# One ScalarE instruction for both PSUM banks of a pair, the first modulation by blocks, a warm-up from a cleared tile, and new instruction orders

## The chip, the core and the metric

The kernel runs on one core of a Trainium2 chip. The metric is device time in microseconds (us) of one execution. A core has five engines that run side by side and meet at semaphores: TensorE (PE, matmuls), VectorE (DVE), ScalarE (ACT), GpSimd (POOL) and SyncE (SP, which issues most DMAs). Matmul results land in PSUM, which has 8 banks of 512 float32 columns for each of 128 partitions.

## The reference

One transformer block on 2048 tokens of width 512, modulated by a condition `c`: Infini-attention (32 heads of 16, four segments of 512 tokens, causal softmax inside a segment plus a linear memory of the earlier ones), and a squared-ReLU feed-forward part of width 1792.

```python
mod = silu(c) @ w_mod                       # sa, ca, ga, sb, cb, gb
h = layernorm(x) * (1 + ca) + sa
q, k, v = heads(h @ wq), heads(h @ wk), heads(h @ wv)
for s in range(4):                          # segments of 512 tokens
    p = softmax(q_s @ k_s.T * 0.25 + causal)
    a_mem = phi(q_s) @ M / (phi(q_s) @ z + 1e-6)
    o_s = g * a_mem + (1 - g) * (p @ v_s)
    M, z = M + phi(k_s).T @ v_s, z + sum(phi(k_s))
x = x + ga * (o @ wo)
h = layernorm(x) * (1 + cb) + sb
x = x + gb * (relu(h @ w1 + b1) ** 2 @ w2 + b2)
```

## The kernel before

The work is cut into 16 units: segment `s` and a quarter `cc` of the heads (8 heads, 128 columns of q and k), `u = 4 s + cc`. For each unit there are q and k (`qk`), for each segment v (`vproj`), then for each of two quads of four heads the row maxima (`a_quad`), the scores, their exponentials and the product with v (`b_quad`), and the memory (`mem`). The output projection (`wo_tile`) and the feed-forward part (`ffn1`, `ffn2`) follow. Operands are split into a high and a low part, and three matmuls stand for one.

Every piece of work is a node of a class `Plan`: an engine, a duration that the author guessed, the nodes it waits for, and the buffers that it takes (`get`) and gives back (`put`). `Plan.run` walks through the nodes in virtual time and so fixes which buffer a key has (`slot`) and at which virtual time a node starts; where a table `ORDER` names the nodes of an engine in sequence, that sequence is kept. The program is then written in the order of the virtual start times. What really waits for what is decided later, from the tiles that the instructions read and write: a semaphore wait is set wherever an instruction and an earlier one of another engine touch the same place. PSUM is handed out by `slot`, banks 0 to 7; the bank of a key is a tile of its own:

```python
def bank(key):
    if key not in TL:
        TL[key] = ps.tile([P, 512], F32, name=f"b{key[0]}", tag=f"bank{PL.slot[key]}")
    return TL[key]
```

TensorE works on half of its rows at a time in `qk`, `vproj`, `a_quad` and the scores: two matmuls of 64 rows run beside each other and write to two banks, a pair. ScalarE reads the two banks of a pair with two instructions: the exponentials (L1081), the copy of the first maxima (L942), the negated maxima (L976), the memory's reads (L1001, L1014) and v (L863, by 128 columns). VectorE takes the maxima in PSUM, in place (L909).

At the start TensorE multiplies a tile `msk` with itself (46 warm-up matmuls, `bwarm`, L562). The modulation's first two rows come by `mod_cols(1, ...)` (L584, L604, L606) and `mod_first(0, ...)` (L619, L625); the first layer norm (`ln1`) applies its statistics (L645), turns the tiles (L654), scales them by the modulation (L666, L668) and splits them into `HT`, from which the first `qk` reads (L782).

Of the kernel before, what the change touches and what calls it, by code (L numbers as in the profile page):

```python
# [8 lines left out]
F32 = mybir.dt.float32  # L9
# [9 lines left out]
P = 128  # L19
# [53 lines left out]
1107 1375 1229 1376 1121 1116 1045-1047 1399 1140 1400 1143 1401-1402 1134 1147 1404 1155 1242 1405 1126 1406 1150
1237 1407 1248 1137 1159 1234 1163 1160-1161 1253 1166 1539 1170 1540 1178 1271 1541-1542 1239 1471 1173 1544-1546
1244 1258 1547 1433 1446 1182-1184 1274 1277 1261 1284 1961-1962 1973-1974 1292 1416-1417 1256 1418-1419 1287 1280
1421 1263 1422 1452 1441 1423 1438 1424 1608 1460 1296-1298 1457 1300 1676 1307 1677 1303 1443 1678-1679 1310 1465
1315 1681-1682 1448 1683 1462 1475 1684 1570 1319 1478 1320-1321 1481 1578 1813 1488 1814 1491 1815 1467 1816 1589
1583 1484 1818-1819 1602 1496 1745 1820 1575 1612 1821 1580 1500 1615 1599 1504 1501-1502 1511 1597 1514 1585 1507
1519 1882 1707 1594 1523 1618 1717 1621 1524-1525 1625 1604 1720 1628 1712 1749 1633 1715 1726 1637-1639 1739 1641
1983 1648 1984 1656 1985 1722 1986 1651 1644 1734 1988-1989 1844 1990 1857 1991 1849 1752 1660-1662 2011 1852 2012  # L80
1755 2013-2014 1762 1765 1854 2016-2017 1770 1731 2018 1859 2019 1736 1863 2145-2146 1873 2083 2147-2148 1758 1876
1868 2150-2151 1741 2152-2153 2045 1871 1774-1776 1778 2028 1781 2029 1785 1788 2030-2031 1793 1878 2033 2064 2058
1797-1799 2034 1892 1899 2050 2035-2036 2053 1907 2273-2275 2055 1902 2276 2211 1895 2077 2278-2280 2069 2060 2281
2074 2192 1911-1913 1915 1922 2072 1918 2205 1930 1925 2079 2197 1934 2200 2173 2087 1935-1936 2094 2097 2401 2178
2402-2404 2102 2183 2090 2406-2407 2186 2408-2409 2181 2339 2106 2188 2110 2113 1886 2107 2117 2202 2120 2108 1889
2301 2125 2309 2129 2215 2314 2218 2130-2131 2207 2311 2222 2225 2320 2230 2325 2234 2467 2235-2236 2306 2238 2241
2550-2552 2330 2245 2248 2553 2561-2564 2316 2253 2328 2429 2333 2257-2259 2439 2335 2343 2350 2346 2627-2630 2358
2434 2353 2362 2437 2448 2583-2586 2594-2595 2366 2442 2369 2363-2364 2373 2381 2444 2596-2597 2376 2456 2572-2573
2461 2453 2385-2387 2458 2471 2574-2575 2463 2474 2478 2481 2605-2606 2486 2490 2494 2497 2491-2492 2501 2504 2509
2607 2637-2638 2649-2650 2616 2608 2617 2513-2515 2618-2619 2863 2881 2803-2805 2865 2806 2867 2781 2868 2782-2783  # L90
2871 2784 2873-2874 2814-2815 2883 2816 2792 2817 2793 2885 2794-2795 2886 2990 2994 2989 2889 2891-2892 2899 2993
2992 2996 2991 2995 2901 2903 2845-2847 2855 2848 2856-2857 2904 2858 2907 2998-2999 2909-2910 3002 2825-2826 2917
2827-2828 3000 2919 2997 2921-2922 3001 2925 3004 2935 3003 3007 2927-2928 2937 2835-2838 3008 3005 2939 3006 3011
2940 2943 3012 3015 3066-3067 3009 2945-2946 2953 2955 3013 3016 3010 3080 2957 3020 2958 3081 3019 3017 2961
2963-2964 3014 2971 3021 3018 3022 3025 3024 2973 3023 3028 2975-2976 3106 3027 2979 3026 2981-2982 3029 3108 3030
3032 3110-3111 3042 3130 3033 3031 3039 3114 3036 3116-3117 3132 3134 3046-3047 3135 3048 3045 3049 3052 3055 3154
# [24 lines left out]
812-813 815 956 814 811 816 810 817 711 868 867 875 874 883 882 853-854 877 975 878 976 871 870 1207 1362 1209 1354
# [120 lines left out]
class Plan:  # L242
# [1386 lines left out]
```

## Time and profile before

| | |
|---|---|
| time, median of 3 runs | 771.0 us (767.26 to 775.83) |
| profiled execution | 772.31 us |
| its span, first to last instruction | 769.6 us |
| mean granted TensorE clock | 0.984 |
| busy: PE / DVE / ACT / POOL | 741.1 / 597.5 / 503.0 / 253.9 us |
| matmuls; ScalarE instructions | 6107; 977 |
| first `qk` matmul | 23.97 us |

The profile names instructions by line, engine, operation, and the tiles they write and read (`bpb<-ST`). Its first part gives the busy time of each engine, its chain the work that ended last, followed back from the end. A row of the groups has the count, busy time, mean nanoseconds of one, and the idle time ahead of it. Ends of matmuls are modelled, so that overlapping ones count once in a busy time and with their full length in a mean.

### The profile page before, as it was taken

The numbers are of one execution on the slowest core, as the hardware profiler recorded it, in microseconds if no ns is written. First come the engines' busy times: TensorE is split into PE (matmuls) and PEld (weight loads), VectorE is DVE, ScalarE is ACT, GpSimd is POOL, SyncE is SP. The second block draws the span as 40 slices with busy tenths as digits, with TensorE's granted clock in tenths as the row PEclk, the third lists the DMA queues.
The fourth block names the chain that finished last, engine by engine and source line by source line (L and its number), as shares of the span: only waits on it lengthen the run. The fifth ranks groups of instructions, "written<-read, shape, count | busy, mean of one in ns | idle before, by whom it ended". The sixth has DMA issues, their size and how long they took to land.

```text
span 769.6 us, 17112 instructions
## 1 busy us (share of the span) xinstructions
PE 741.1 (96%) x6107; PEld 579.8 (75%) x6107; DVE 597.5 (78%) x1459; ACT 503.0 (65%) x977; POOL 253.9 (33%) x351
## 2 busy tenths in 40 slices
PE   8999999999999999999999699999999999999998
PEld 4777657875777658765566478898999898899886
DVE  4585788978987878588778989999968776687542
ACT  1547778888887896788868445666657455645441
POOL 4445355457665674464667230100000000000000
PEclk9999899999999999999999799999999999999999
DMA  9664757446565766658887858655543243243401
GB/s 303 164 163 113 217 182 204 133 131 167 181 172 159 189 175 173 181 142 209 241 232 232 251 186 256 215 172 179 150 150 116 99 123 110 77 136 96 151 1 55
DMA packets 102141, 126.69 MB, mean 165 GB/s; under 512 B 18981, under 2 KB 54569, under 8 KB 102058
## 3 DMA queue, kind: packets, MB, share of 16 engines
q1 hardware_dynamic: 101906, 125.49, 55.9%
q8 instruction: 48, 0.79, 0.4%
q14 instruction: 35, 0.29, 0.1%
q10 hardware_dynamic: 152, 0.13, 0.1%
HBM read 70.59 MB, written 27.99 MB: 128 GB/s over the span
## 4 chain that ended last, share of the span: by engine, by line
PE 77%; DMA 6%; ACT 6%; SPq 4%; DVE 3%; issue 2%; POOL 1%; DVEq 0%; ACTq 0%; POOLq 0%
PE bqk L792 7%; PE bpf L1573 7%; PE bpf L1572 7%; PE bpf L1571 7%; PE bpv L1123 6%; PE bv L871 6%; PE ba L904 5%; PE bpb L1064 5%; PE bhy L1510 3%; PE bhy L1512 3%; PE bhy L1511 3%; ACT pt L1081 3%; SPq L846 3%; PE bhx L1510 2%; PE bhx L1512 2%; PE bhx L1511 2%
## 5 line engine op out<-in xcount | busy, mean ns | idle before, releaser
L909 DVE CUSTOM_DVE_ANT_0 ba<-ba,msk 128x384 f32<-128x384 f32 (+2 forms) x384 | 185.8, 542 | 48.1 <-PE ba L904 43.4
L1081 ACT ACTIVATE pt<-bpb 128x512 f32<-128x512 f32 x320 | 169.7, 610 | 20.3 <-PE bpb L1064 17.6
L792 PE MATMUL bqk<-HT,WQK 64*128 64x512 f32 x720 | 100.8, 396 | 0.6 <-POOL hinge_s L526 0.6
L1068 POOL TENSOR_SCALAR_AFFINE_SELECT pt<-pt 128x512 f32<-128x512 f32 x128 | 80.1, 649 | 49.2 <-ACT pt L1081 40.9
L1571 PE MATMUL bpf<-W,ST 128*128 128x512 f32 x224 | 89.1, 398 | 0.3 <-ACT ST L1555 0.3
L1573 PE MATMUL bpf<-W,ST 128*128 128x512 f32 x224 | 88.8, 396 | 0.5 <-DVE ST L1558 0.5
L1572 PE MATMUL bpf<-W,ST 128*128 128x512 f32 x224 | 88.7, 396 | 0.0
L1456 ACT CAST ST<-SG 128x768 fp32r<-128x768 f32 (+1 forms) x56 | 51.9, 940 | 54.5 <-PE bhy L1511 51.0
L1064 PE MATMUL bpb<-ST 64*128 64x256 f32 (+2 forms) x512 | 79.9, 353 | 5.7 <-ACT pt L1081 1.8
L904 PE MATMUL ba<-ST 63*128 63x256 f32 (+2 forms) x512 | 78.2, 355 | 3.9 <-DMA ST<-SG 1.3
L792 PEld LDWEIGHTS bqk<-HT,WQK 64*128 64x128 f32 x720 | 72.8, 185 | 10.2 <-POOL hinge_s L526 1.0
L1123 PE MATMUL bpv<-pt,VT 128*32 128x512 f32 (+3 forms) x1024 | 78.8, 437 | 0.7 <-POOL pt L1068 0.6
L1064 PEld LDWEIGHTS bpb<-ST 64*128 64x128 f32 x512 | 52.1, 188 | 26.3 <-ACT pt L1081 7.4
L904 PEld LDWEIGHTS ba<-ST 63*128 63x128 f32 x512 | 51.8, 188 | 25.8 <-ACT pt L1081 9.0
L1459 DVE TENSOR_TENSOR ST<-SG,ST 128x768 fp32r<-128x768 f32 (+1 forms) x56 | 61.2, 1098 | 7.1 <-ACT ST L1456 7.1
L1209 POOL TENSOR_TENSOR X1L<-X1L 128x512 f32<-128x512 f32 x40 | 52.8, 1323 | 27.6 <-DMA X1L<-o_gate 22.8
L1549 ACT ACTIVATE AC<-AC,b1c 128x512 f32<-128x512 f32 x56 | 38.1, 718 | 28.8 <-DVE AC L1531 28.6
L871 PE MATMUL bv<-WVO,HT 64*128 64x512 f32 x384 | 56.0, 399 | 0.6 <-DVE xt L668 0.4
L1123 PEld LDWEIGHTS bpv<-pt,VT 128*32 128x32 f32 x1024 | 27.8, 109 | 36.8 <-issue 25.6
L909 DVE DVE_READ_ACCUMULATOR2_ANT mx<- 128x1 f32 x384 | 53.6, 140 | 0.0
L1558 DVE TENSOR_TENSOR ST<-AC,ST 128x1024 fp32r<-128x1024 f32 x28 | 34.2, 1222 | 21.2 <-ACT ST L1555 21.1
L1573 PEld LDWEIGHTS bpf<-W,ST 128*128 128x128 f32 x224 | 42.1, 188 | 10.9 <-DVE ST L1558 1.0
(201 smaller groups left out, 1710.0 us busy)
## 6 DMA issues: line engine op xcount, KB each, us to landing
ST<-SG SPq DMA_DIRECT2D x192, 128.0 KB
SG<-s_dram SPq DMA_DIRECT2D x21, 512.0 KB
SG<-in_B_w SPq DMA_DIRECT2D x35, 256.0 KB
o_raw<-oraw SPq DMA_DIRECT2D x16, 512.0 KB
X1L<-o_raw SPq DMA_DIRECT2D x28, 256.0 KB
X1L<-o_gate SPq DMA_DIRECT2D x28, 256.0 KB
wm<-in_w_mod SPq DMA_DIRECT2D x20, 256.0 KB
xt<-in_A_x SPq DMA_DIRECT2D x16, 256.0 KB
```

The source lines that it names most:

```text
L792: m = nc.tensor.matmul(bank(("qk", u, w)), W3(w, k, x, cc * P, (cc + 1) * P)[z], HT[z, y, k], start=(ph == 0 and k == 0 and i == 0), stop= ...
L871: m = nc.tensor.matmul(bank(("v", s, t)), HT[z, x, k, t * P:(t + 1) * P], WVO[z, k, y], start=(ph == 0 and k == 0 and i == 0), stop=(ph == ...
L904: nc.tensor.matmul(dst[:, c0:c0 + n], ST[b:b + 63, 0, sl, qt * P:(qt + 1) * P], ST[b:b + 63, 1, sl, :n], start=True, stop=True)
L909: nc.vector.tensor_tensor_reduce(i, i, msk[:, 512 - n:], scale=1.0, scalar=-3e38, op0=ALU.add, op1=ALU.max, accum_out=o)
L1064: nc.tensor.matmul(dst, ST[b:b + 64, 1, sl, kb * P:(kb + 1) * P], ST[b:b + 64, 0, sl, q0:512], start=True, stop=True)
L1068: nc.gpsimd.affine_select(out=ap, in_=ap, pattern=[[0, ap.shape[1]], [1, P]], compare_op=ALU.is_ge, fill=0.0, base=0, channel_multiplier=-1)
L1081: ns = [act(512, lambda j=j: nc.scalar.activation(buf("PPP"[n], pt)[:, i + j], bank(keys[j]), AF.Exp, scale=0.25), pr[slot] + 0.01 + 0.001 ...
L1123: nc.tensor.matmul(bank(o)[32 * hq:32 * hq + 32, q0:q0 + src.shape[1]], v[:, a:a + 32], src, start=start, stop=stop, tile_position=(0, 32 ...
L1459: nc.vector.tensor_tensor(TL[kd][:, 1, o:o + b - a], raw(k)[:, a:b], TL[kd][:, 0, o:o + b - a].bitcast(F32), op=ALU.subtract)
L1571: nc.tensor.matmul(p, rh, FF["W2"][:, f, 0], start=(f == 0), stop=False)
L1572: nc.tensor.matmul(p, rh, FF["W2"][:, f, 1], start=False, stop=False)
L1573: nc.tensor.matmul(p, rl, FF["W2"][:, f, 0], start=False, stop=(f == NF - 1))
```

## The change

All of PSUM becomes one tile `PB` of 8 banks. `bank(key)` is a slice of it, and `banks(keys)` a view of two banks, a slice with the distance of the two as its step. The six reads of a pair by ScalarE become one instruction each. Where a node takes two banks, the lower one goes to the first key.

```diff
+    PB = ps.tile([P, 8, 512], F32, name="PB")
+
     def bank(key):
-        if key not in TL:
-            TL[key] = ps.tile([P, 512], F32, name=f"b{key[0]}", tag=f"bank{PL.slot[key]}")
-        return TL[key]
+        return PB[:, PL.slot[key]]
+
+    def banks(keys):
+        a, b = (PL.slot[k] for k in keys)
+        return PB[:, a:b + 1:b - a]
...
+        two = [key for pool, key in n.get if pool[0] == "#"]
+        if len(two) == 2 and self.slot[two[0]] > self.slot[two[1]]:
...
-            ns = [act(512, lambda j=j: nc.scalar.activation(buf("PPP"[n], pt)[:, i + j], bank(keys[j]), AF.Exp, scale=0.25),
-                      pr[slot] + 0.01 + 0.001 * j, after=[k], put=[keys[j]]) for j in (0, 1)]
+            ns = [act(1024, lambda: nc.scalar.activation(buf("PPP"[n], pt)[:, i:i + 2], banks(keys), AF.Exp, scale=0.25),
+                      pr[slot] + 0.01, after=[k], put=keys)]
...
-        cp = [act(512, lambda j=j: nc.scalar.copy(buf("ac", ac)[:, j], bank(keys[j])), pr[0] + 0.01 + 0.001 * j, after=[first],
-                  put=[keys[j]]) for j in (0, 1)]
+        cp = [act(1024, lambda: nc.scalar.copy(buf("ac", ac), banks(keys)), pr[0] + 0.01, after=[first], put=keys)]
...
-                nc.tensor.transpose(bank(b[r])[:16, z], TL[mx][z], ident[z, z])
+                nc.tensor.transpose(bank(b[r])[:16, 0:64], TL[mx][z], ident[z, z])
```

The same is done to the copies of v (256 columns of two banks), of the memory's reads (two lines) and of the negated maxima. The start and the planner's constants:

```diff
-    RARE, COLD, NEAR, LATE, RING = 2.3, 3.4, 0.12, 0.1, 8
+    RARE, COLD, NEAR, LATE, RING = 1.8, 3.4, 0.12, 0.1, 8
-    FREE = {"PE": 2.0, "ACT": 2.6, "DVE": 2.7, "POOL": 2.4, "SP": 0.8, "NIL": 0.0}
+    FREE = {"PE": 1.2, "ACT": 2.6, "DVE": 2.7, "POOL": 2.4, "SP": 0.8, "NIL": 0.0}
...
+    wz = const.tile([P, P], BF, name="wz")
+    nc.vector.memset(wz, 0.0)
...
-        pe("F", 0.22, lambda: nc.tensor.matmul(bank(wk_), msk[:, :P], msk, start=True, stop=True), 50.0,
+        pe("F", 0.22, lambda: nc.tensor.matmul(bank(wk_).rearrange("p (a n) -> p a n", a=4), wz, wz[:, None, :].to_broadcast([P, 4, P]), start=True, stop=True), 50.0,
...
-    n_ca = mod_cols(1, CA, 1.0, PR0 + 0.1, pool="P")
-    n_sa = mod_first(0, SA, 0.0, PR0 + 0.2)
-    MODC = {CA: [n_ca, n_sa]}
+    def mod_block(j):
+        c = slice(j * P, (j + 1) * P)
+        ld = [sp(lambda m=m: nc.sync.dma_start(buf("P", keys_m[m])[:, :, c],
+                                               wmod[:, m * D + j * P:m * D + (j + 1) * P].rearrange("(k p) n -> p k n", p=P)),
+                 PR0 + 0.1 + 0.01 * j + 0.001 * m, 200000, get=() if j else [("P", keys_m[m])]) for m in (0, 1)]
+        def mm():
+            for m in (0, 1):
+                for k in range(KD):
+                    nc.tensor.matmul(bank(b_m)[:, 2 * j + m:2 * j + m + 1], TL[keys_m[m]][:, k, c], cs[:, k:k + 1],
+                                     start=k == 0, stop=k == KD - 1)
...
+        return dve(2, lambda: nc.vector.tensor_tensor(modc[:, 0:2, j], bank(b_m)[:, 2 * j:2 * j + 2], one, op=ALU.add),
+                   PR0 + 0.13 + 0.01 * j, after=[n], put=[b_m])
+    MODC = {CA: [mod_block(j) for j in range(KD)]}
```

With this the scaling of columns block `k` waits for its own block of the modulation, and the first `qk` group for the first two parts of `HT`, its third step for the others. The tables of `ORDER` are all written anew; they begin

```diff
     "PE": """
-16 43 31 47 22 40 50 44 59 38 3 54 49 57 25 39 35 52 19-20 17 36 61 33 76 42 27 30 46 71 28 21 37 73 34 53 78 48 80 82
+16 29 18 20 45 28 52 39 21 44 59 3 35 55 22 25 61 50 37 36 23 58 49 56 48 32 26-27 38 40 54 51 69 43 46 73 90-91
```

The following rows are the built programs' instructions in sequence, with the semaphores each waits for in brackets (`Activation_49` counts ScalarE's instructions, `DVE_49` VectorE's, `PE_49` TensorE's, `Pool_49` GpSimd's). Before, on TensorE, in segment 0 where q and k of unit 1 (L792), v (L871) and the first maxima (L904) are interleaved:

```order
L871 MATMUL bv<-WVO,HT 128x512 x6
L792 MATMUL bqk<-HT,WQK 128x512 [waits Pool_49]
L792 MATMUL bqk<-HT,WQK 128x512 x5
L871 MATMUL bv<-WVO,HT 128x512 x6
L904 MATMUL ba_710<-ST 128x256 [waits DVE_49]
L904 MATMUL ba_711<-ST 128x256 [waits Activation_49]
```

The change, at the same work (q and k are L798 now, v L877, maxima L909):

```order
L877 MATMUL PB<-WVO,HT 128x512 x6
L909 MATMUL PB<-ST 128x512 [waits Activation_49]
L909 MATMUL PB<-ST 128x512
L798 MATMUL PB<-HT,WQK 128x512 [waits Pool_49]
L798 MATMUL PB<-HT,WQK 128x512 x5
L798 MATMUL PB<-HT,WQK 128x512 [waits Activation_49]
L798 MATMUL PB<-HT,WQK 128x512 x5
L798 MATMUL PB<-HT,WQK 128x512 [waits Activation_49]
L798 MATMUL PB<-HT,WQK 128x512 x5
```

The 48 matmuls of a unit's q and k add into the same two banks; two of its groups of six, in the midst of this sum, now begin with a wait for ScalarE.

On TensorE a little later, where the first scores (L1064, now L1066) come among q and k of the next unit, before:

```order
L904 MATMUL ba_934<-ST 128x512 [waits Activation_49]
L792 MATMUL bqk<-HT,WQK 128x512 [waits Pool_49]
L792 MATMUL bqk<-HT,WQK 128x512 x11
L1064 MATMUL bpb<-ST 128x256 [waits Activation_49] x2
L1064 MATMUL bpb<-ST 128x384 x2
L904 MATMUL ba_967<-ST 128x256 [waits DVE_49]
```

and with the change:

```order
L798 MATMUL PB<-HT,WQK 128x512 x6
L798 MATMUL PB<-HT,WQK 128x512 [waits Activation_49]
L798 MATMUL PB<-HT,WQK 128x512 x5
L909 MATMUL PB<-ST 128x256 x2
L909 MATMUL PB<-ST 128x384 x2
L1066 MATMUL PB<-ST 128x256 x2
```

Here, too, a group of the same sum has a wait for ScalarE that stood nowhere in it before.

On ScalarE, the exponentials of unit 0's first quad, before (L1081 for each bank, beside the copies of v, L863):

```order
L863 COPY VT_150<-bv 128x8x16
L1081 ACTIVATE pt<-bpb 128x512 [waits PE_49]
L1081 ACTIVATE pt<-bpb 128x512 [waits PE_49,Pool_49]
L1081 ACTIVATE pt<-bpb 128x512 [waits PE_49]
L1081 ACTIVATE pt<-bpb 128x512
L1081 ACTIVATE pt<-bpb 128x512 [waits PE_49] x2
```

and with the change (L1083 and L869):

```order
L869 COPY VT_152<-PB 128x16x16 [waits PE_49]
L1083 ACTIVATE pt<-PB 128x1024 [waits DVE_49]
L1083 ACTIVATE pt<-PB 128x1024 [waits DVE_49,PE_49]
L1083 ACTIVATE pt<-PB 128x1024 [waits PE_49]
L1083 ACTIVATE pt<-PB 128x1024 [waits DVE_49,PE_49]
```

Each row of 1024 columns stands for two of 512, and three of these four wait for VectorE besides, which none of the rows before does.

More of the change, by code (lines that the diff above doesn't have):

```diff
@@ L313, in run @@
             heapq.heappush(ev, (free[e], k, None, 0))
-        k, todo, idle, cold, rare = 0, len(self.nodes), free["PE"], 0.0, 0.0
+        k, todo, idle, cold, rare = 0, len(self.nodes), free["PE"], self.START, 0.0
         while todo:
@@ L607, in mod_cols @@
                    pr + 0.05, after=[n], put=[b])
-    def mod_first(m, slot, plus, pr):
-        key, b = ("wmod", m), ("modc", m)
-        n = None
-        for k in range(KD):
-            ld = sp(lambda k=k: nc.sync.dma_start(buf("P", key)[:, k], wmod[k * P:(k + 1) * P, m * D:(m + 1) * D]),
-                    pr + 0.001 * k, 175000, get=() if k else [("P", key)])
-            def mm(k):
-                for j in range(KD):
-                    nc.tensor.matmul(bank(b)[:, KD * j + k:KD * j + k + 1], TL[key][:, k, j * P:(j + 1) * P], cs[:, k:k + 1],
-                                     start=True, stop=True)
-            n = pe("F", 0.9, lambda k=k: mm(k), pr + 0.02 + 0.001 * k, after=[n_cs, ld, n], get=() if k else [("#D", b)],
-                   put=[key] if k == KD - 1 else (), act=0.05)
-        def out_():
-            nc.vector.tensor_reduce(modc[:, slot, :], bank(b)[:, :KD * KD].rearrange("p (j k) -> p j k", k=KD), axis=AX.X, op=ALU.add)
-            if plus:
-                nc.vector.tensor_scalar(modc[:, slot, :], modc[:, slot, :], plus, None, op0=ALU.add)
-        return op("DVE", 0.15 if plus else 0.08, out_, pr + 0.05, after=[n], put=[b])
     def ln_stats(xt, mv):
@@ L649, in ln_transposed, with need @@
         b = [("lnq", sc, s, i, j) for j in (0, 1)]
+        def need(k):
+            return MODC[sc][k:k + 1] if sc == CA else MODC[sc]
         def turn(h):
@@ L697, in block_kernel @@
     load_x(0, PR0)
-    n_ca = mod_cols(1, CA, 1.0, PR0 + 0.1, pool="P")
-    n_sa = mod_first(0, SA, 0.0, PR0 + 0.2)
-    MODC = {CA: [n_ca, n_sa]}
+    one = const.tile([P, 2], F32, name="one")
+    nc.vector.memset(one[:, 0:1], 0.0)
+    nc.vector.memset(one[:, 1:2], 1.0)
+    n_blk = []
+    keys_m, b_m = [("wm", 0, 0), ("wm", 1, 0)], ("modc", 0)
+    def mod_block(j):
[8 more added lines that the diff above has]
+                                     start=k == 0, stop=k == KD - 1)
+        n = pe("F", 0.9, mm, PR0 + 0.12 + 0.01 * j, after=[n_cs, *ld], get=() if j else [("#D", b_m)], put=keys_m, act=0.05)
+        if j == 0:
+            n_blk.append(n)
+        else:
+            n_blk[0].outs.append(n)
+            n.left += 1
+        return dve(2, lambda: nc.vector.tensor_tensor(modc[:, 0:2, j], bank(b_m)[:, 2 * j:2 * j + 2], one, op=ALU.add),
+                   PR0 + 0.13 + 0.01 * j, after=[n], put=[b_m])
+    MODC = {CA: [mod_block(j) for j in range(KD)]}
     HTN = {}
@@ L887, in vproj @@
             HUSE[s].append(n)
-            for t in (t0, t0 + 1):
-                for cc in range(4):
-                    u = 4 * s + cc
-                    VN[u].append(act(128, lambda t=t, cc=cc: cp(t, cc), pr[t] + 0.02 + 0.001 * cc,
-                                     after=[n, *VUSE[u - NV], *(VTN[u:u + 1])], put=[("v", s, t)]))
+            for cc in range(4):
+                u = 4 * s + cc
+                VN[u].append(act(256, lambda t0=t0, cc=cc: cp(t0, cc), pr[t0] + 0.02 + 0.001 * cc,
+                                 after=[n, *VUSE[u - NV], *(VTN[u:u + 1])], put=[("v", s, t0), ("v", s, t0 + 1)]))
     MXN = {}
@@ L973, in turn_m @@
                 z = slice(64 * r, 64 * r + 64)
-                nc.tensor.transpose(bank(b[r])[:16, z], TL[mx][z], ident[z, z])
+                nc.tensor.transpose(bank(b[r])[:16, 0:64], TL[mx][z], ident[z, z])
         n = pe("R", 0.06, turn_m, p_tail, after=reds, get=[("#D", k) for k in b], put=[mx])
-        n = [act(64, lambda r=r: nc.scalar.mul(buf("mt", mt, F32R)[:, 64 * r:64 * r + 64], bank(b[r])[:16, 64 * r:64 * r + 64], -1.0),
-                 p_tail, after=[n], get=() if r else [("mt", mt)], put=[b[r]]) for r in (0, 1)]
+        n = [act(128, lambda: nc.scalar.mul(buf("mt", mt, F32R).rearrange("p (r n) -> p r n", r=2), banks(b)[:16, :, 0:64], -1.0),
+                 p_tail, after=[n], get=[("mt", mt)], put=b)]
         sl = (4 * u + 2 * qd) % NSLOT
@@ L1000, in mem @@
             MRD[u] = [n]
-            n = [act(512, lambda r=r: nc.scalar.copy(buf("oraw", ar)[:4 * VP, r], bank(bs[r])[:4 * VP, :]), pr[0] + 0.01, after=[n], put=[bs[r]])
-                 for r in (0, 1)]
+            n = [act(1024, lambda: nc.scalar.copy(buf("oraw", ar)[:4 * VP], banks(bs)[:4 * VP]), pr[0] + 0.01, after=[n], put=bs)]
             AMN[u] = sp(lambda: nc.sync.dma_start(o_raw[u][2 * P:].rearrange("(r p) n -> p r n", r=2), TL[ar][:4 * VP]), pr[0] + 0.02, 290000, lat=1.35,
@@ L1013, in mem @@
             n = pe("R", 0.24, tr, pr[2], after=[PHN[u, 1], PKN.get(u - 1)], get=[("#D", k) for k in b] + [("pk", pk)], put=[f])
-            n = [act(256, lambda r=r: nc.scalar.copy(buf("pk", pk).rearrange("p (t n) -> p t n", t=4)[:, :, 64 * r:64 * r + 64],
-                                                     bank(b[r])[:, 0:256].rearrange("p (t n) -> p t n", t=4)), pr[2] + 0.01,
-                     after=[n], put=[b[r]]) for r in (0, 1)]
+            n = [act(512, lambda: nc.scalar.copy(buf("pk", pk).rearrange("p (t r n) -> p r t n", t=4, r=2),
+                                                 banks(b)[:, :, 0:256].rearrange("p r (t n) -> p r t n", t=4)), pr[2] + 0.01, after=[n], put=b)]
             def upd():
```

283 lines of the change are left out of this document (129 added, 154 removed), and 36 rows, old and new, of the table ORDER.

## The prediction

> **What bounds the kernel now.** I read the page's busy shares and its chain first, then busy time by stretches, then the chain inside one stretch.
>
> ```profile
> PE 741.1 (96%) x6107; PEld 579.8 (75%) x6107; DVE 597.5 (78%) x1459; ACT 503.0 (65%) x977; POOL 253.9 (33%) x351
> ...
> PE 77%; DMA 6%; ACT 6%; SPq 4%; DVE 3%; issue 2%; POOL 1%; DVEq 0%; ACTq 0%; POOLq 0%
> ```
>
> TensorE is busy for 96% of the span; the chain runs through it for 77%, through ScalarE for 6% (46 us), VectorE for 3% and GpSimd for 1%: 77 us in the three that wait for PSUM or feed TensorE.
>
> ```profile
> core 0: us, PE busy (x) PEld busy (x) DVE busy (x) ACT busy (x) POOL busy (x), PEclk, DMA share, GB/s
> 24.00:460.00 436.00, 414.95 (x4128) 296.31 (x4127) 351.62 (x1066) 325.49 (x733) 242.46 (x323) 0.98 0.66 183
> 460.00:740.00 280.00, 279.56 (x1746) 249.93 (x1745) 225.10 (x357) 164.77 (x226) 3.42 (x4) 1.00 0.45 142
> ```
>
> From 460 us on there is the feed-forward part: TensorE idles 0.4 us in 280. No instruction there reads two banks, so I take it as unchanged. What the change can move lies in the start (24 us) and the attention (24 to 460 us), where TensorE idles 21 us and ScalarE 110 us. In a middle stretch of the attention, 130 to 160 us, the chain is this:
>
> ```profile
> by line: PE bv L871 25.9%; PE bpv L1123 21.0%; PE bqk L792 18.8%; PE ba L904 12.5%; PE bpb L1064 10.1%; PE blnq L654 6.8%; PE bmr L997 2.6%; PE bmu L1022 1.0%; PE bpkt L1012 0.8%; PE bat L974 0.7%; issue 0.1%
> ...
> 141.55 1.38 PE bqk L792 x12
> ```
>
> It has nothing but TensorE in it. There a shorter ScalarE instruction gains nothing, and any time for which TensorE stands still is added to the end. Twelve half-row matmuls, six pairs, take 1.38 us: 0.23 us for a pair.
>
> **ScalarE's reads.** What they cost now, and the rows from which I take a read of 1024 columns:
>
> ```profile
> L1081 ACT ACTIVATE pt<-bpb 128x512 f32<-128x512 f32 x320 | 169.7, 610 | 20.3 <-PE bpb L1064 17.6 <-PE bat L974 0.6 <-PE ba L904 0.5
> ...
> L942 ACT COPY AC<-ba 128x512 f32<-128x512 f32 x64 | 36.9, 603 | 17.3 <-PE ba L904 17.1
> ...
> L1555 ACT CAST ST<-AC 128x1024 fp32r<-128x1024 f32 x28 | 29.5, 1052 | 3.9 <-PE bpf L1572 2.7 <-PE bwop L1265 0.5
> ...
> L1147 ACT COPY oraw<-bpv 128x512 f32<-128x512 f32 x32 | 19.1, 596 | 13.9 <-PE bpv L1123 9.9 <-ACT AC L942 2.0 <-issue 1.0
> ...
> L1001 ACT COPY ar<-bmr 80x512 f32<-80x512 f32 x24 | 13.7, 594 | 2.7 <-PE bmr L997 2.7
> L863 ACT COPY VT<-bv 128x128 f32<-128x128 f32 x64 | 13.5, 302 | 5.4 <-PE bv L871 2.8 <-PE ba L904 2.6
> L976 ACT ACTIVATE mt<-bat 16x64 fp32r<-16x64 f32 x64 | 10.3, 202 | 8.3 <-PE bat L974 7.7 <-ACT HT L674 0.4
> L1524 ACT COPY u<-bhx 128x256 f32<-128x256 f32 x28 | 10.2, 368 | 20.0 <-PE bhx L1512 15.4 <-DVE AC L1531 3.6 <-DVE ST L1297 1.0
> ...
> L1014 ACT COPY pk<-bpkt 128x256 f32<-128x256 f32 x24 | 8.4, 387 | 2.8 <-PE bpkt L1012 2.5
> ```
>
> Reads of PSUM take 368 ns for 256 columns and 596 for 512: 0.89 ns a column, so 596 + 456 = 1052 ns for 1024. The row of 1024 columns out of SBUF says the same. No row shows a read of two banks; it lies between 1.05 us and two single ones, 1.22 us. I take 1.05. ScalarE then saves 160 x (1.22 - 1.05) = 27 us on the exponentials, and in the same way 5 on L942, 5 on L976, 6 on L863, 2 each on L1001 and L1014: **47 us of its 325** in the attention. As seen, hardly any of that is on the path.
>
> [...]
>
> **What the one tile adds.** The order rows in the section on the change show waits for ScalarE in the midst of sums that TensorE is adding up, in banks that ScalarE doesn't read. I followed every wait in the built program to the instruction that ends it, and compared the banks. 280 ScalarE instructions read two banks; 55 pairs are neighbours, 225 have other banks between. The view with a step is treated as all banks from the first to the last. So 172 matmuls wait for a read whose two banks lie on either side of theirs, each for another read; 141 reads wait for a matmul in such a bank, 93 for VectorE, and 92 VectorE instructions wait for such a read. The program before has none of these.
>
> The price of one: TensorE does what stands between, then stops until the read is over.
>
> ```profile
> L792 PE MATMUL bqk<-HT,WQK 64*128 64x512 f32 x720 | 100.8, 396 | 0.6 <-POOL hinge_s L526 0.6
> ...
> 14.27 0.59 ACT L588 COPY t<-bmod 128x512 f32<-128x512 f32 x1 [6.16 <-PE bmod L584]
> ...
> 14.91 1.05 PE L604 MATMUL bmodc<-selc,t 128*128 128x1 f32 x8
> ```
>
> A matmul of 512 columns takes 0.396 us, but the next pair may start after 0.23: its result comes 0.17 us later than TensorE is free. The copy L588 ends at 14.86, and the matmul that needs it starts at 14.91: 0.05 us. So a long read holds TensorE for 0.17 + 1.05 + 0.04 = 1.26 us after the matmul that it waited for, less the work that stands between. Of the 172, 149 have such a matmul among the read's own waits, and the work between, at 0.23 us a pair of 512 columns (and in proportion), is:
>
> - under 0.25 us (0.05 on average) in 102 cases, 85 with a long read: 85 x 1.21 = 103 us, and 17 short reads (0.26 to 0.6 us, priced alike) 9 us;
> - 0.25 to 0.5 us in 19: 16 us; 0.5 to 0.75 in 16: 8 us; 0.75 to 1 in 7: 3 us; over 1 us in 5: nothing.
>
> Sum: **+138 us**. The same arithmetic on the waits for ScalarE in the program before, bank by bank, gives 7 us: there the work between covers the reads. Bounds: with the 1.05 us of the read alone and the first two groups, 85 x 1.0 + 17 x 0.4 + 13 = 105; at its full price, all 149, 188.
>
> The other 23 waits have no matmul to count from; each costs 0 to 1.26 us: 0 to 29, taken as 14. VectorE's share:
>
> ```profile
> L909 DVE CUSTOM_DVE_ANT_0 ba<-ba,msk 128x512 f32<-128x512 f32 x128 | 86.4, 711 | 21.6 <-PE ba L904 21.3
> ...
> L909 DVE DVE_READ_ACCUMULATOR2_ANT mx<- 128x1 f32 x384 | 53.6, 140 | 0.0
> ```
>
> A read that waits for a maximum waits up to 0.71 + 0.14 us; 92 x 0.85 = 78 us at most, and nothing where the maximum was over. It reaches the end only through a matmul that waits for that read. I take a quarter, 19.
>
> What goes away: a TensorE that stands still for over 150 us lets the waits that the chain now has in ScalarE, VectorE and GpSimd run out unseen: 0 to 77 us. Part of the 77 lies outside the attention, and part has PE at work beside it; I take a little under half: -35.
>
> **The start.**
>
> ```profile
> 12.42 1.05 POOL L642 TENSOR_TENSOR mv<-mv,mhalf 128x4 f32<-128x4 f32 x1
> ...
> 16.00 0.16 DVE L606 TENSOR_SCALAR modc<-bmodc 128x4 f32<-128x4 f32 x1 [4.06 <-PE bmodc L604]
> 16.08 3.25 DVE L645 TENSOR_SCALAR xt<-xt,mv 128x512 f32<-128x512 f32 x4
> ```
>
> The statistics are done at 13.47 us, but VectorE reaches L645 only at 16.08, behind the modulation's L606. In the new order the four L645 stand ahead of the modulation's four small sums: 2.6 us earlier, and each block of `HT` needs only its own block. The loads become 8 of 256 KB as before, in rows of 512 bytes where they were 2 KB. Bounds: -5 (a block's wait less besides) to +1 us (loads late); I take **-3**. The earlier warm-up gains nothing alone, since the first `qk` waits for `HT`. The other moves of the orders I put at nothing, with TensorE's 21 us of idle time as the bound to both sides; changes between full-row, half-row and column tiling on TensorE are 131 before and 140 now.
>
> **The sum**, against the profiled execution's own 772.3 us (1.3 above the median of 771.0): 772.3 + 138 + 14 + 19 - 35 - 3 = **905 us**.
>
> **The rivals.**
>
> *The waits are there but don't hold anything*, faster. For it: a wait costs nothing where the read is over when the matmul comes, and TensorE runs up to a stalled group with little loss now (idle 21 us of 436). Against it: 102 waits with 0.05 us between. ScalarE's part of the chain would shrink by 47/325, 7 us, the start by 3, and up to half of TensorE's idle time, 10, might go: 772 - 20 = **752**. It decides where the work between exceeds 1.26 us, which it does in 5 of 149. [...]
>
> *They take the place of what TensorE waits for now.* If all 77 us of the chain in the other engines run out, and the reads cost 0.5 us each, 149 x 0.5 = 75: **no change, 772**. Against it: a long read alone lasts 1.05.
>
> *All three engines in lockstep*: the waits of VectorE and ScalarE at full price, 772 + 138 + 29 + 78 - 10: **1007**. Against it: VectorE has 84 us idle in the attention, and more once TensorE stops.
>
> *Slower, but with more of it absorbed*: 772 + 105 - 60 - 3: **814**.
>
> **How the numbers follow.** Forecast 0.82; waits that hold nothing 0.04; no change 0.03; lockstep 0.06; more absorbed 0.05. The range for 8 in 10 runs from 105 + 14 + 5 - 56 - 5 = +63 (835) to 138 + 29 + 60 - 15 + 1 = +213 (985); it leaves out the ends of the last two rivals and the two that aren't slower. A measurement spreads from 767.3 to 775.8, so 1% is about what it can tell from no change. Faster by over 1%: 0.04; within: 0.03; slower: 0.93.
>
> **What will show it.** Of the waits before, these are the largest of TensorE for the exponentials:
>
> ```profile
> PEld ba L904 <- ACT pt L1081: 9.0, 14, 1.7
> ...
> PEld bpb L1064 <- ACT pt L1081: 7.4, 18, 1.3
> ```
>
> With the change, L1083 with 160 instructions of about 1.05 us; ScalarE under 470 us busy; among the waits, TensorE (its weight loads too) for L1083 with some 100 us, where these two have 16; ScalarE's share of the chain well over 6%; TensorE's busy share near 80%; the first `qk` at about 21 us; 280 us for the feed-forward part as before. Wrong would be a read of two banks far from 1.05 us; TensorE's waits for L1083 that stay near 16 us (then the waits were over in time); or stalls long enough that the granted clock, now 0.984, falls, which would add to the sum and isn't in it.

## The result and the profile after

| | before | changed |
|---|---|---|
| time, median of 4 runs each | 771.3 us (767.3 to 775.8) | 976.2 us (971.7 to 984.7) |
| profiled execution, span | 772.3, 769.6 us | 972.7, 971.0 us |
| granted TensorE clock | 0.984 | 0.928 |
| ScalarE instructions | 977 | 696 |

The ratio is 1.264, with a 95% interval of 1.258 to 1.270: **slower by 205 us**. The forecast was 905 us, slower by 133, with a range of 835 to 985 us. The measured time lies inside the range, near its upper end; the direction and the waits came out as written, and some 70 us were missing from the sum.

The page of the changed kernel: busy times (PEld stands for TensorE's loads of weights), the clock by slices of 24 us, the chain, and the row of the exponentials.

```profile
PE 804.2 (83%) x6123; PEld 584.4 (60%) x6123; DVE 602.1 (62%) x1464; ACT 499.2 (51%) x696; POOL 251.8 (26%) x351
...
PEclk9997787999797998798989798979999999999999
...
PE 69%; ACT 17%; DVE 7%; issue 3%; DMA 2%; POOL 1%; SPq 0%; ACTq 0%; DVEq 0%; POOLq 0%
...
L1083 ACT ACTIVATE pt<-PB 128x1024 f32<-128x1024 f32 x160 | 162.2, 1023 | 132.3 <-DVE mx L914 31.3 <-PE PB L1066 27.7 <-PE PB L798 21.8
```

ScalarE, the engine with 281 instructions fewer, has gone from 6% of the chain to 17%. TensorE's idle time is 971.0 - 804.2 = 166.8 us, where it was 28.5. Its busy time rose as well, by 63 us, with only 16 matmuls more: the clock row shows 7s and 8s all through the attention. So 138 us of the loss is TensorE at rest, and 63 us is TensorE busy for longer. The exponentials waited 31 us for the maxima (`DVE mx`) and 22 us for q and k (L798); the row of before names neither.

The waits (who waits, for whom: us in total, times, longest) that answer to the two of before, 9.0 and 7.4 us:

```profile
PEld PB L1066 <- ACT pt L1083: 50.7, 36, 3.2
...
PE PB L1066 <- ACT pt L1083: 36.2, 32, 3.0
...
PEld PB L909 <- ACT pt L1083: 31.2, 24, 2.5
...
PE PB L909 <- ACT pt L1083: 19.9, 22, 2.2
...
PE PB L798 <- ACT pt L1083: 14.6, 14, 1.7
```

Scores (L1066), maxima (L909) and the sums of q and k (L798) wait for exponentials. One such wait in the order of time, on TensorE and then on ScalarE (start, length, and in brackets the idle time before it):

```profile
116.76 1.56 PE L798 MATMUL PB<-HT,WQK 64*128 64x512 f32 x7
119.26 0.73 PE L798 MATMUL PB<-HT,WQK 64*128 64x512 f32 x4 [0.94 <-ACT pt L1083]
```

```profile
118.18 1.02 ACT L1083 ACTIVATE pt<-PB 128x1024 f32<-128x1024 f32 x1 [1.77 <-PE PB L798]
```

The read waits for a matmul of q and k, which writes a bank that the read doesn't want, and starts at 118.18, as TensorE ends its work there. The next matmul of the same sum waits for the read, which ends at 119.20, and starts at 119.26: TensorE rests for 0.94 us, nearly the whole length of a read of the scores, in a sum of q and k.

By stretches, in the columns of before:

```profile
core 0: us, PE busy (x) PEld busy (x) DVE busy (x) ACT busy (x) POOL busy (x), PEclk, DMA share, GB/s
24.00:640.00 616.00, 457.00 (x4003) 279.33 (x4002) 333.74 (x1025) 309.38 (x434) 236.24 (x328) 0.89 0.45 122
640.00:940.00 300.00, 297.09 (x1845) 265.91 (x1846) 244.79 (x392) 174.63 (x241) 9.32 (x9) 0.99 0.47 149
```

A matmul of the feed-forward stretch takes TensorE 297.09 / 1845 = 0.161 us, where it was 279.56 / 1746 = 0.160: this part is what it was. Its first matmul (L1512, L1510 before) came at 427.3 us and comes at 633.1 now, 206 us later. So all of the loss lies ahead of it, in the attention, at a clock of 0.89.

### The profile page after: what moved, and what is told of

The parts are those of the page before. It is cut to its first block, busy times and chain, and to the rows that moved or that the text cites. A ratio compares the mean times of both kernels' runs of the same rounds, so it can differ in the third digit from the quotient of the medians.

```text
span 971.0 us, 16752 instructions
## 1 busy us (share of the span) xinstructions
PE 804.2 (83%) x6123; PEld 584.4 (60%) x6123; DVE 602.1 (62%) x1464; ACT 499.2 (51%) x696; POOL 251.8 (26%) x351
## 4 chain that ended last, share of the span: by engine, by line
PE 69%; ACT 17%; DVE 7%; issue 3%; DMA 2%; POOL 1%; SPq 0%; ACTq 0%; DVEq 0%; POOLq 0%
ACT pt L1083 12%; PE PB L798 7%; PE PB L1125 7%; PE PB L1573 5%; PE PB L1575 5%; PE PB L909 5%; PE PB L1574 5%; PE PB L1066 5%; PE PB L1512 5%; PE PB L1514 5%; PE PB L1513 5%; PE PB L877 4%; DVE PB L914 4%; ACT AC L947 2%; PE PB L1266 1%
## 5 line engine op out<-in xcount | busy, mean ns | idle before, releaser
L914 DVE CUSTOM_DVE_ANT_0 PB<-PB,msk 128x384 f32<-128x384 f32 (+2 forms) x384 | 187.5, 542 | 205.9 <-PE PB L909 108.2
L1083 ACT ACTIVATE pt<-PB 128x1024 f32<-128x1024 f32 x160 | 162.2, 1023 | 132.3 <-DVE mx L914 31.3
L798 PE MATMUL PB<-HT,WQK 64*128 64x512 f32 x720 | 117.0, 426 | 19.5 <-ACT pt L1083 14.6
L1066 PE MATMUL PB<-ST 64*128 64x256 f32 (+2 forms) x512 | 85.0, 383 | 42.9 <-ACT pt L1083 36.2
L909 PE MATMUL PB<-ST 63*128 63x256 f32 (+2 forms) x512 | 89.3, 400 | 31.1 <-ACT pt L1083 19.9
L1125 PE MATMUL PB<-pt,VT 128*32 128x512 f32 (+3 forms) x1024 | 92.2, 482 | 17.9 <-ACT pt L1083 11.1
L798 PEld LDWEIGHTS PB<-HT,WQK 64*128 64x128 f32 x720 | 74.1, 199 | 38.5 <-ACT pt L1083 18.5
L909 PEld LDWEIGHTS PB<-ST 63*128 63x128 f32 x512 | 54.9, 215 | 70.0 <-ACT pt L1083 31.2
L1066 PEld LDWEIGHTS PB<-ST 64*128 64x128 f32 x512 | 51.0, 206 | 74.7 <-ACT pt L1083 50.7
L1573 PE MATMUL PB<-W,ST 128*128 128x512 f32 x224 | 89.5, 399 | 0.0
L1574 PE MATMUL PB<-W,ST 128*128 128x512 f32 x224 | 88.4, 395 | 0.0
L1575 PE MATMUL PB<-W,ST 128*128 128x512 f32 x224 | 88.4, 395 | 0.0
L877 PE MATMUL PB<-WVO,HT 64*128 64x512 f32 x384 | 60.7, 428 | 9.5 <-ACT pt L1083 7.1
L1512 PE MATMUL PB<-H2a,ST 128*128 128x256 f32 x196 | 55.6, 284 | 0.2 <-DVE AC L1533 0.2
L1514 PE MATMUL PB<-H2a,ST 128*128 128x256 f32 x196 | 55.6, 284 | 0.0
L1513 PE MATMUL PB<-H2a,ST 128*128 128x256 f32 x196 | 55.6, 283 | 0.0
```

What stands on the lines that cost most here:

```text
L798: m = nc.tensor.matmul(bank(("qk", u, w)), W3(w, k, x, cc * P, (cc + 1) * P)[z], HT[z, y, k], start=(ph == 0 and k == 0 and i == 0), stop= ...
L909: nc.tensor.matmul(dst[:, c0:c0 + n], ST[b:b + 63, 0, sl, qt * P:(qt + 1) * P], ST[b:b + 63, 1, sl, :n], start=True, stop=True)
L914: nc.vector.tensor_tensor_reduce(i, i, msk[:, 512 - n:], scale=1.0, scalar=-3e38, op0=ALU.add, op1=ALU.max, accum_out=o)
L1066: nc.tensor.matmul(dst, ST[b:b + 64, 1, sl, kb * P:(kb + 1) * P], ST[b:b + 64, 0, sl, q0:512], start=True, stop=True)
L1083: ns = [act(1024, lambda: nc.scalar.activation(buf("PPP"[n], pt)[:, i:i + 2], banks(keys), AF.Exp, scale=0.25), pr[slot] + 0.01, after=[k] ...
L1125: nc.tensor.matmul(bank(o)[32 * hq:32 * hq + 32, q0:q0 + src.shape[1]], v[:, a:a + 32], src, start=start, stop=stop, tile_position=(0, 32 ...
```

## The experiments

**Splitting the reads again.** In the first kernel every read of two banks becomes two instructions at the same place; the one tile, the start and the orders stay:

```diff
+    def parts(keys, what):
+        a, b = (PL.slot[k] for k in keys)
+        if False:
+            return [(slice(0, 2), banks(keys))]
+        return [(slice(r, r + 1), PB[:, i:i + 1]) for r, i in enumerate((a, b))]
...
-            ns = [act(1024, lambda: nc.scalar.activation(buf("PPP"[n], pt)[:, i:i + 2], banks(keys), AF.Exp, scale=0.25),
-                      pr[slot] + 0.01, after=[k], put=keys)]
+            ns = [act(1024, lambda: [nc.scalar.activation(buf("PPP"[n], pt)[:, i + r.start:i + r.stop], z, AF.Exp, scale=0.25)
+                                     for r, z in parts(keys, "pt")], pr[slot] + 0.01, after=[k], put=keys)]
```

> All 280 reads of two banks are emitted as two instructions of one bank each, at the same place; the one PSUM tile, the start and the orders stay. In the built program none of the 512 waits across banks is left. Theory (those waits cost the time): 755 to 785 us, granted clock back to 0.97 or more, TensorE's waits for the exponentials under 25 us instead of some 100. Rival 1 (the new orders or the start are at fault): still above 930 us. Rival 2 (a single tile for PSUM costs time even where each read names one bank): above 850 us.

Measured: **766.0 us** (764.4 to 767.3), where the kernel before took 773.8 beside it, a ratio of 0.9915 (0.9887 to 0.9942). Its page, and its largest waits of TensorE for the exponentials (L1094 there):

```profile
PE 739.8 (97%) x6123; PEld 577.0 (76%) x6123; DVE 599.5 (79%) x1464; ACT 500.0 (66%) x976; POOL 252.0 (33%) x351
```

```profile
PEld PB L1077 <- ACT pt L1094: 7.0, 24, 0.8
PEld PB L916 <- ACT pt L1094: 4.8, 9, 0.8
```

The whole loss is gone, idle time is back at 22.9 us and the clock at 0.984. Orders, start and the one tile are cleared; the wide view alone costs 976.2 - 766.0 = 210 us.

**Doses.** With the same helper, only the exponentials are split (`if what != "pt"`), or all but the exponentials (`if what == "pt"`).

> Only the 160 exponentials are split, the other 120 reads stay on two banks: 58 of the 172 waits of TensorE in the midst of other banks remain, with reads of 0.27 to 1.0 us behind them. Theory by count: of the 204 us lost, 204 x 58/172 = 69 remain, 841 us; less where the remaining reads are short, so 800 to 845. Rival (orders or start): above 930. If the loss grows faster than the count because the clock falls with the stalls, it lies under 820.

> The reverse: only the 160 exponentials read two banks at once, the other reads are split: 120 of 172 waits of TensorE remain, all behind reads of 1.02 us. Theory by count: 772 + 204 x 120/172 = 914 us, 880 to 940, clock between 0.93 and 0.96. Rival (orders or start): above 930, as with every other kernel of this set. Rival (the losses of the groups don't add, one stall hides in another): the loss here and that of the kernel with split exponentials sum to well over or under 204 us.

Measured: 814.3 us (809.4 to 816.4; clock 0.971) and **921.8 us** (920.6 to 928.6; clock 0.925). Both lie in the ranges of the theory by count and far from the rivals' (the clock of the second a little under its 0.93). Over the split kernel that is 48 and 156 us, together 204 of the 210: the two groups of waits add, neither hides in the other, and what is left, 6 us, is no more than the runs spread.

**Neighbouring banks.** `take` gives a node with two banks the pair of free neighbours that has been free the longest, and a node with one bank a bank without free neighbours:

```diff
+        near = [q for q in free if q + 1 in free]
+        if want == 2 and near:
+            q = min(near, key=lambda q: max(free.index(q), free.index(q + 1)))
+            for i in (q + 1, q):
+                free.insert(0, free.pop(free.index(i)))
+        elif want == 1:
+            q = min(free, key=lambda q: ((q - 1 in free) + (q + 1 in free), free.index(q)))
+            free.insert(0, free.pop(free.index(q)))
```

Once all reads are wide; once only those of neighbours (`if b == a + 1`); once none.

> All 280 reads take two banks in one instruction as in the changed kernel, but a pair is given neighbouring banks where two are free: 211 pairs are neighbours, 69 are not, and 46 of 172 waits of TensorE across banks are left, with 26 of 185 between ScalarE and VectorE. Theory by count: 766 + 210 x 46/172 = 822 us, 800 to 835, and less of a fall of the clock (0.96 to 0.98). Rival (the wide read itself is at fault, not the banks between): still above 930.

> A pair is given neighbouring banks where two are free (211 of 280 pairs, 55 without this), and only neighbours are read by one instruction; the other 69 are read by two. No wait across banks is left. Theory (only the banks between cost time, the wide read does not): 750 to 780 us. Rival (a wide read by itself holds its banks too long, since the first is free only after 1.02 us instead of 0.6): 785 to 830. Rival (orders or start): above 930.

> Neighbouring banks as before, but every read of one bank: against the kernel that reads neighbours at once (764.3 us) it has the same banks and 211 more instructions on ScalarE. Theory (ScalarE is off the path): within 1% of it, 758 to 772 us. Rival (fewer instructions on ScalarE do shorten the time): 3 to 10 us above it, 768 to 775.

Measured, all three in the range of the theory: all wide 815.5 us (812.5 to 820.2; clock 0.977); neighbours wide **764.3 us** (763.6 to 770.7), ratio 0.9895 (0.9861 to 0.9929); none wide 761.9 us (758.7 to 769.7), ratio 0.9856 (0.9816 to 0.9896). In the order of dose:

| kernel | TensorE's waits across banks | us | over the split kernel | for each wait |
|---|---|---|---|---|
| all split | 0 | 766.0 | | |
| all wide, near banks | 46 | 815.5 | 49.5 | 1.08 |
| exponentials split | 58, mostly short reads | 814.3 | 48.3 | 0.83 |
| exponentials wide | 120, all long | 921.8 | 155.7 | 1.30 |
| the change | 172 | 976.2 | 210.2 | 1.22 |

The waits were counted in the built programs. The time follows their number and the length of the reads. The mean clock of the profiled executions is 0.984, 0.977, 0.971, 0.925 and 0.928, in the order of the table. In the trace of the change the clock is 0.50 for 140 us and 1.00 for the rest; if the others have the same two steps, their means stand for 24, 37, 47 and 139 us at 0.50, by this estimate. So the part of the loss that is the clock doesn't grow with the count alone: it jumps between 58 and 120 waits. A read of two banks does no harm where its banks are neighbours, and no measurable good either (764.3 us against 761.9). What 211 wide reads save on ScalarE is seen between the pages of the kernel with no wide reads and the one with wide neighbours, and in the exponentials' rows:

```profile
PE 744.8 (97%) x6123; PEld 584.0 (76%) x6123; DVE 598.4 (78%) x1464; ACT 499.9 (65%) x976; POOL 251.9 (33%) x351
...
L1103 ACT ACTIVATE pt<-PB 128x512 f32<-128x512 f32 x320 | 167.9, 614 | 25.3 <-PE PB L1086 18.4 <-POOL e L859 2.2 <-POOL X1L L1231 1.3
```

```profile
PE 741.8 (96%) x6123; PEld 580.9 (76%) x6123; DVE 599.6 (78%) x1464; ACT 490.3 (64%) x765; POOL 252.8 (33%) x351
...
L1103 ACT ACTIVATE pt<-PB 128x1024 f32<-128x1024 f32 (+1 forms) x203 | 160.9, 850 | 30.8 <-PE PB L1086 26.4
```

It is 9.6 us, 0.045 us for a pair, off the path. These two kernels and the split one are 0.9 to 1.4% below the one before, with intervals that leave out 1 and overlap: which of them is best stays open.

**The price of one wait by itself.** The split kernel, with pauses put into the feed-forward part, where TensorE otherwise rests for 0.2 us in 298: a small GpSimd instruction waits for the second matmul of a group, and the third waits for it (`swap(h, [m2])` makes `h` wait for `m2`). Nothing stands between. Sparse and short:

```diff
+            if (4 * f + t) % 7 == 0:
+                h = nc.gpsimd.tensor_tensor(hold, hold, hold, op=ALU.add)
+                swap(h, [m2])
+                swap(m3, [h])
```

The dense pauses have `% 2` in place of `% 7`. The long ones have a tile `hold` of 8 columns and this line instead:

```diff
+                h = nc.gpsimd.tensor_tensor(hold[:, 0:4], hold[:, 0:4], hold[:, 4:8], op=ALU.pow)
```

> The kernel with all reads split (766.0 us), and in the feed-forward part, where TensorE never waits, 32 pauses (one in about 9 us): the third matmul of every seventh group of the second layer is made to wait for a small GpSimd instruction (4 columns, about 1.04 us) that itself waits for the second matmul. It measures the price of one wait by itself. Theory: 0.17 us until the matmul's result is there, 1.04 and 0.05 to 0.1: 1.26 to 1.31 us each, 766 + 41 = 807 us, and a granted clock that stays at 0.98 or more, since the pauses are far apart. Rival (a pause costs much less, other work fills it): under 790. Rival (each pause also slows what follows, at any distance): over 825.

> The same with 112 pauses, one for every second group, one in about 2.7 us of work, nearly as dense as the waits across banks lie in the attention of the changed kernel (172 in about 450 us of work). Theory A (a pause costs its own length and no more): 766 + 112 x 1.27 = 908 us, clock unchanged. Theory B (pauses this dense also lower the granted clock, which is what the forecast left out): clock in the feed-forward part under 0.93 and 925 to 960 us, and the busy time of TensorE itself grows by 20 to 50 us with the same work.

> The 32 sparse pauses with a longer GpSimd instruction (a power of 4 columns, 1.04 us in other lines, where the sum took 0.37 on average): 22.7 us were lost with the short one, 0.71 each, so 0.34 besides the instruction. Theory: 766 + 32 x (0.34 + 1.04) = 810 us, 1.4 us for each, against the forecast's 1.26 for a read of 1.05. The clock stays at 0.98 or more. Rival (a long pause costs no more than a short one): 790.

> The 112 dense pauses with the longer instruction: a pause of about 1.5 us after 2.7 us of work, so TensorE stands for a third of the time, as it does in the attention of the changed kernel at its worst. With the price of the sparse pauses alone: 766 + 112 x 1.4 = 923 us and a clock of 0.98. If pauses as long and as dense as these make the clock fall (the short ones at the same places did not: 0.99 in this part): clock under 0.95, TensorE's busy time up by 30 to 60 us, 950 to 985 us.

| pauses | GpSimd instruction, mean us | us | over 766.0, for each pause | clock, whole profiled execution |
|---|---|---|---|---|
| 32 short | 0.37 | 788.7 (785.5 to 793.1) | 0.71 | 0.991 |
| 112 short | 0.36 | 860.4 (857.6 to 866.3) | 0.84 | 0.974 |
| 32 long | 1.14 | 817.1 (815.4 to 820.9) | 1.59 | 0.975 |
| 112 long | 1.14 | 982.2 (980.5 to 982.6) | 1.93 | 0.932 |

The sum of 4 columns took 0.37 us and not the 1.04 that I had taken from a line with a power, so the first two numbers expected were too high, and 788.7 fell under the 790 of the rival for this reason. Theory B failed for the short pauses: no time of 925 us or more, and no clock under 0.93. With the longer instruction the sparse pauses came to 817 us (810 expected) and the dense ones to 982, in the range that goes with a falling clock and far above 766 + 112 x 1.59 = 944. The feed-forward part of the split kernel, then with dense short, sparse long and dense long pauses (columns as above):

```profile
460.00:758.00 298.00, 297.82 (x1844) 265.65 (x1843) 228.82 (x359) 170.01 (x232) 2.54 (x4) 1.00 0.41 129
```

```profile
460.00:850.00 390.00, 328.75 (x1845) 259.40 (x1843) 234.41 (x365) 171.49 (x234) 43.11 (x113) 0.99 0.32 101
```

```profile
460.00:800.00 340.00, 299.59 (x1805) 258.42 (x1805) 228.91 (x359) 166.81 (x229) 38.15 (x36) 0.99 0.36 113
```

```profile
460.00:960.00 500.00, 355.36 (x1838) 280.46 (x1837) 231.40 (x359) 171.59 (x233) 126.47 (x113) 0.91 0.24 77
```

By matmul (the stretches hold 1805 to 1845 of them) TensorE is busy for 0.162, 0.178, 0.166 and 0.193 us, at a clock of 1.00, 0.99, 0.99 and 0.91. So the short pauses alone make it busy for 31 us more, 0.28 us each, at nearly the full clock; the 27 us that the long dense ones add to this go with the clock of 0.91. How it goes down is seen in the dense one, on TensorE:

```profile
602.90 0.39 PE L1586 MATMUL PB<-W,ST 128*128 128x512 f32 x1
603.13 0.39 PE L1587 MATMUL PB<-W,ST 128*128 128x512 f32 x1
604.73 0.50 PE L1588 MATMUL PB<-W,ST 128*128 128x512 f32 x1 [1.21 <-POOL hold L1590]
605.07 0.40 PE L1586 MATMUL PB<-W,ST 128*128 128x512 f32 x1
605.30 0.39 PE L1587 MATMUL PB<-W,ST 128*128 128x512 f32 x1
606.90 0.50 PE L1588 MATMUL PB<-W,ST 128*128 128x512 f32 x1 [1.21 <-POOL hold L1590]
...
609.49 0.63 PE L1586 MATMUL PB<-W,ST 128*128 128x512 f32 x1
609.91 0.63 PE L1587 MATMUL PB<-W,ST 128*128 128x512 f32 x1
```

and on GpSimd for the first of the two pauses, with TensorE's waits for all of them (in total, times, longest):

```profile
603.67 1.01 POOL L1590 TENSOR_TENSOR hold<-hold 128x4 f32<-128x4 f32 x1 [8.91 <-PE PB L1587]
...
PE PB L1588 <- POOL hold L1590: 150.6, 112, 2.1
```

Two pauses with 1.21 us of idle time follow each other; two and a half microseconds after the second, a matmul of 512 columns takes 0.63 us and the next starts after 0.42 instead of 0.23. The first alone had left the next at 0.23 (605.07, 605.30). The long sparse pauses show the slow pace too:

```profile
465.56 0.79 PE L1588 MATMUL PB<-W,ST 128*128 128x512 f32 x1 [1.21 <-POOL hold L1590]
...
467.43 0.63 PE L1279 MATMUL PB<-WVO,ST 128*128 128x512 f32 x1
467.85 0.63 PE L1280 MATMUL PB<-WVO,ST 128*128 128x512 f32 x1
...
471.69 0.40 PE L1587 MATMUL PB<-W,ST 128*128 128x512 f32 x1
471.92 0.39 PE L1588 MATMUL PB<-W,ST 128*128 128x512 f32 x1
```

Behind this pause matmuls of 512 columns start 0.42 us apart, and 0.23 again from 471.69 on. Over their whole 340 us the clock is 0.99, which with steps of 1.00 and 0.50 is some 7 us at 0.50, by this estimate: most of the 32 pauses left it alone. In the dense one, the first pause of the rows also shows the price at full clock: L1588 comes 1.60 us after L1587, 1.37 more than the usual 0.23, and the matmul behind it 0.34 after, 0.11 more. That is 1.48 us, with a GpSimd instruction of 1.01 us in it, so 0.47 besides it. With the mean instruction of 1.14 us this gives 1.61 us, near the 1.59 of the sparse long pauses.

## Why the prediction was right, and what it left out

- **The time**: 976.2 us lies in the range, 71 us above the forecast. It also lies only 31 us below the 1007 of the lockstep rival. The range held it in part by luck: its upper end is made of a larger share of VectorE, of the 23 other waits, and of less that is absorbed, but the largest part of what was missing is, by the estimate below, the clock, which the range left out as well.
- **What bounds the kernel, and where the change acts**: right. The loss lies in the attention, and the feed-forward part kept its 0.16 us for a matmul. The sparse long pauses cost 1.59 us for an instruction of 1.14 us, so stops of TensorE do go to the end in full there. For the attention this wasn't measured by itself.
- **The wide view names every bank between**: right, and shown by taking away the wide view (766.0) and by taking away only the banks between (764.3). The rival in which the waits hold nothing is out.
- **The clock, the term left out.** The forecast said that stalls long enough for the granted clock to fall "would add to the sum", and put nothing for them. The clock fell from 0.984 to 0.928. In the changed kernel it stood at 0.50 in 21 stretches of 3.4 to 13.6 us, 140 us together, in which TensorE was busy for 113.6; in the kernel before, whose mean of 0.984 is also the split kernel's, in 4 stretches, 24 us together, busy for 20.7. At half clock the matmuls of 512 columns above start 0.42 us apart instead of 0.23, so 45% of the busy time is lost, and the clock's share is, by this estimate, 0.45 x (113.6 - 20.7) = 42 us of the missing 71. One of these stretches, and the time behind it:

```profile
250.90:261.10 10.20, 7.63 (x65) 4.34 (x66) 2.97 (x7) 4.41 (x6) 3.03 (x5) 0.50 0.53 152
261.10:271.00 9.90, 8.60 (x88) 5.79 (x88) 6.39 (x20) 5.76 (x7) 1.67 (x6) 1.00 0.44 127
```

  That stops of TensorE bring the clock down is shown by the long dense pauses in the feed-forward part (0.91, where the split kernel has 1.00); that they are the reason in the attention too is carried over from there. The built program told how dense the stops would be, 172 of up to 1.26 us in the 415 us of work of the attention, one for each 2.4 us; no row of before told what stops as dense as that do to the clock.
- **The price of a wait, 0.17 + 1.05 + 0.04 = 1.26**: too low. Three steps for ScalarE can be read in the changed kernel:

```profile
122.69 0.50 PE L1066 MATMUL PB<-ST 64*128 64x512 f32 x2 [0.93 <-ACT pt L1083]
123.03 1.55 PE L798 MATMUL PB<-HT,WQK 64*128 64x512 f32 x12
```

```profile
121.61 1.02 ACT L1083 ACTIVATE pt<-PB 128x1024 f32<-128x1024 f32 x1
123.24 1.03 ACT L1083 ACTIVATE pt<-PB 128x1024 f32<-128x1024 f32 x1 [0.60 <-PE PB L1066]
```

  The first read ends at 122.63 and TensorE starts 0.06 later; the pair behind it starts after 0.34 instead of 0.23, 0.11 more; the pair's result is there at 123.19 and the next read starts 0.05 later. With these, a long read costs 0.17 + 0.05 + 1.02 + 0.06 + 0.11 = 1.41 us. The start of the read after the matmul and the slow restart were not in the 1.26. (GpSimd took 0.15 where ScalarE takes 0.05: 603.52 to 603.67.) On the 85 long reads the 0.15 us more are 13 us, on all 149 waits 22 us.
- **The waits as a sum, 138 + 14 + 19 - 35 = 136**: too low; some 166 us by the runs. Against the split kernel the span grew by 971.0 - 762.7 = 208 us, and 42 of these are the clock, by the estimate above. The longer price makes up 13 to 22 of the 30 us between. How much of the 166 is VectorE's share, the 23 others, or old waits absorbed was not told apart. VectorE's share of the chain rose from 3% (23 us) to 7% (68 us), and the exponentials' 31 us of waiting for the maxima are new, so 19 us may be too little. The part of the lockstep rival that has VectorE's waits at full price is not ruled out by any run. (The listed terms of the 138 add to 139.)
- **ScalarE saves 47 us**: wrong in size. From the split kernel to the change its busy time went from 500.0 to 499.2, and with wide neighbours to 490.3; under 470 was expected. The read's length was right (1.05 forecast, 1.02 measured), but I multiplied the mean of a single read, 0.61 us, by two. Two reads in a row overlap: 167.9 us for 320 is 0.525 each, 1.05 for a pair, and the 169.7 us in the row of before said the same. A mean in a row of the groups holds the overlap twice; the busy time over the count does not. It cost nothing here, since it was off the path.
- **The start, -3**: the first `qk` matmul came at 20.73 us (23.97 before), 3.2 us earlier. **The orders, 0 with 21 to both sides**: start and orders together are worth -7.7 us (ratio 0.9915), and no run separates them.

## What to carry to other kernels

Before two reads are joined into one with a step, look at what the view is taken for by whoever sets the waits: here it was everything from the first bank to the last, and 172 waits on the bounding engine came of it. Join reads only where the banks are neighbours, and expect a gain only on an engine that is on the path (9.6 us less of ScalarE, off the path, gave none here). When a forecast adds pauses to TensorE, price each with its whole round trip (here 0.17 us to the result, 0.05 and 0.06 for the hand-overs, the instruction's own time, 0.11 for the slow restart), and add the clock. Here it fell to 0.89 and 0.91 where TensorE rested for 26% (159 of 616 us, the attention) and 29% (145 of 500, long dense pauses) of a stretch, and it kept 0.99 at 12% (long sparse) and 16% (short dense).

## What was not expected of the hardware

- Pauses decide on the clock by their length and density together: 112 with 0.36 us of GpSimd work left the feed-forward part at 0.99, the same 112 with 1.14 us took it to 0.91, and 32 of those left it at 0.99. Behind two of 1.21 us of idle time, 2.2 us apart, matmuls of 512 columns started 0.42 us apart; behind the first of the two alone it was 0.23.
- The clock comes in steps: in the stretch from 250.9 to 261.1 us it is 0.50, and 1.00 in the 10 us behind it. In the traces of the kernel before and of the change it is one or the other all through.
- A pause costs TensorE busy time as well: 0.28 us for each short one at a clock of 0.99. By the rows of the long ones, the slow restart is 0.11 of it and the last result, which nothing covers, 0.39 - 0.23 = 0.16.
- Two reads of 512 columns in a row cost ScalarE 1.05 us, one read of 1024 columns in two banks 1.02: nearly no gain in joining them.
